# Q's zero-padded parity copies of two token groups: by GpSimd multiplies or by DMA into standing zeros

## The chip, the cores and the metric

The kernel runs on one core of one Trainium2 chip. The metric is the device time of one execution in microseconds (us), as a median of several. A profile is one further execution, recorded by the hardware profiler.

A core has engines that run side by side, each with its own queue of instructions: TensorE (PE; its weight loads stand apart as PEld), VectorE (DVE), ScalarE (ACT), GpSimd (POOL), and SyncE (SP), which here only issues DMA transfers. An engine takes its instructions strictly in order. An instruction that must wait for another engine or a transfer holds up all that stand behind it on its engine.

## What is computed

One transformer block with conditioning: a sliding-window attention branch, then a branch that mixes tokens, each behind a LayerNorm that is modulated from a vector c. There are 2048 tokens with 512 features, and the attention has 32 heads of 16 features and a window of 256.

```python
mod = (_silu(c) @ w_mod).reshape(c.shape[0], 6, 1, -1)
sa, ca, ga, sb, cb, gb = (mod[:, 0], ..., mod[:, 5])
h = _layernorm(x) * (1 + ca) + sa
# attention branch A(h)
q, k, v = (h @ wqkv) split into 32 heads of 16
scores = einsum('bhqd,bhkd->bhqk', q, k) * 16 ** -0.5
scores = where(0 <= i - j < 256, scores, -1e9)
o = einsum('bhqk,bhkd->bhqd', softmax(scores), v)
x = x + ga * (o @ wo)
h = _layernorm(x) * (1 + cb) + sb
# token-mixing branch B(h), with its own layernorm
u = gelu(einsum('bsd,sf->bdf', layernorm(h), w1) + b1)
y = einsum('bdf,fs->bds', u, w2) + b2
x = x + gb * y^T
```

## The kernel before

**Tiling.** The 2048 tokens are cut into four token groups of 512 (`tg` 0 to 3), the 32 heads into four head groups of eight (`g8` 0 to 3). A head group's Q and K are kept transposed: 128 rows (8 heads of 16 features) by 512 tokens. Attention for one token group and head group takes five units: two of kind A for the even heads, here called units 0 and 1 of the head group, one of kind C (unit 2) with the far and near corners of the window for all eight heads, and two of kind A for the odd heads. In a token group units count 5 x g8 + k, from 0 to 19.

**Why Q is there twice.** A score matmul contracts 32 rows (one of four strips of a tile, `tile_position`), and 32 rows are two heads. So that only one head counts, Q is kept in a tile `QT[tg][g8]` of 128 rows by two copies by 512 tokens: copy 0 holds the even heads with zeros in the rows of the odd ones, copy 1 the reverse. K needs no such copy. `emit_scores` (L538) reads copy 0 for the even heads, copy 1 for the odd heads, both in unit 2.

**How QT is made.** TensorE multiplies `wqkv` with `h1T` into PSUM (`dense`, L267, its matmuls bear the line L271). VectorE copies the result into a bf16 tile `qs` (L309; two buffers in turn). Then GpSimd multiplies `qs` by `mask_even` and by `mask_odd`, columns of ones and zeros by row, into the two copies (L313). The tile is allocated anew for each Q block, from a pool with two buffers for each head group. The first block of all (L511 to L523) and one half of the second are made by VectorE.

**The other pieces around it.** V goes into `VaugT` (L287), with a column of ones beside each head. The products of unit 2's probabilities read V from `Vc`, in which keys are shifted by half a block. SyncE fills it with transfers within SBUF (`copy_vc`, L631; `copies_for`, L637): two or three per head group, sent at the ends of units 0, 3, 4 and 5 of a token group. The matmuls that read it are L623. While the attention runs, SyncE also loads the first half of `w1` (`w1a`, one piece per unit from token group 1, each paced behind an exponential, L408).

**What sets the order.** The schedule is written out by hand, unit by unit (L881 to L914): the exponential of unit u (ScalarE, L598), the scores of unit u + 1, then the products of unit u - 1, and one group of dense work from `plan` (L760) whose result VectorE evacuates. Q blocks of the next token group are computed in units 13 (head group 0) and 17 (head group 1) of the group before, and those of head groups 2 and 3 in units 3 and 5 of their own. Scores are needed one unit ahead of the unit's exponential. LayerNorm steps and the like come as chains that `fill` (L723) places in VectorE's free time by a clock that the planner keeps for each engine; `evac`'s return value, 1.4 us for a Q block, tells it how long GpSimd is taken by the two multiplies (`on_pool`, L719). After the attention come the token-mixing matmuls on TensorE (L964, L1050, L1086).

Of the kernel before, what the change touches and what calls it, by code (L numbers as in the profile page):

```python
# [8 lines left out]
DT = mybir.dt  # L9
# [3 lines left out]
P = 128  # L13
# [3 lines left out]
DH = 16  # L17
# [3 lines left out]
ND = D // P  # L21
# [9 lines left out]
def kernel(  # L31
# [25 lines left out]
    dma = nc.sync  # L57
# [107 lines left out]
    build_masks()  # L165


    qpool = tc.alloc_tile_pool(name="qpool", bufs=2)
    kpool = tc.alloc_tile_pool(name="kpool", bufs=1)
    vpool = tc.alloc_tile_pool(name="vpool", bufs=1)  # L170
    qspool = tc.alloc_tile_pool(name="qspool", bufs=2)
# [7 lines left out]
    QT = [[None] * ND for _ in range(NG)]  # L179
# [13 lines left out]
    nc.gpsimd.memset(ones[:], 1.0)  # L193


    for tg in range(NG):
        VaugT[tg] = Vring[tg % 2]
        for g8 in range(ND):
            KT[tg][g8] = Kring[tg % 2][:, g8, :]

# [66 lines left out]
    def dense(out, lhsT, rhs, start, stop):  # L267

        for j in range(4):
            cols = slice(32 * j, 32 * j + 32)  # L270
            nc.tensor.matmul(  # L271
                out[cols, :], lhsT=lhsT[:, cols], rhs=rhs, start=start, stop=stop,
                tile_position=(0, 32 * j), skip_group_check=True,
            )
# [17 lines left out]
    def qk_group(tg, g8, kind, pool):  # L292
        col0 = g8 * P + (D if kind == "k" else 0)

        def mms():
            pq = pool.tile([P, 4 * P], DT.float32, name="dn")
            for dc in range(ND):
                dense(
                    pq, lhsT=wqkv[:, dc, col0 : col0 + P], rhs=h1T[tg][:, dc, :],
                    start=(dc == 0), stop=(dc == ND - 1),  # L300
                )
            return pq

        def evac(pq):
            if kind == "k":
                nc.vector.tensor_copy(out=KT[tg][g8], in_=pq[:])  # L306
                return
            qs = qspool.tile([P, 4 * P], DT.bfloat16, name="qs")
            nc.vector.tensor_copy(out=qs[:], in_=pq[:])  # L309
            QT[tg][g8] = qpool.tile([P, 2, 4 * P], DT.bfloat16, name=f"QT{g8}")  # L310
            for n, m in enumerate((mask_even, mask_odd)):
                eng = nc.vector if (tg, g8, n) == (0, 1, 0) else nc.gpsimd
                eng.tensor_scalar(  # L313
                    out=QT[tg][g8][:, n, :], in0=qs[:], scalar1=m[:], scalar2=0.0, op0=ALU.mult, op1=ALU.add,
                )
            return 0.7 if (tg, g8) == (0, 1) else 1.4
        return mms, evac, (1.05 if (tg, g8, kind) == (0, 1, "q") else 0.7)
# [70 lines left out]
    with tc.manual_schedule():  # L388
# [6 lines left out]
            out=spread[:].rearrange("p (a b) -> p a b", a=4),  # L395
            in_=identity[0:32, 0:32].unsqueeze(1).to_broadcast([32, 4, 32]),
# [52 lines left out]
        for lo, hi, in_ in (  # L449
# [3 lines left out]
                out=mask_q[:, lo:hi, :], in_=in_.to_broadcast([P, hi - lo, 64]), func=ACT.Copy,  # L453
            )
        for half in range(2):
            part64 = slice(64 - 64 * half, 128 - 64 * half)
            nc.scalar.activation(
                out=Vc[half][part64, :, 0:8, :], func=ACT.Copy,
                in_=zero[part64, 0 : 8 * 2 * DH].rearrange("p (h d) -> p h d", d=2 * DH)
# [32 lines left out]
        for dc in range(ND):  # L492
            if dc < 2:
                nc.vector.tensor_scalar(
                    out=h1T[0][:, dc, :], in0=pts[dc], scalar1=modFM[:, 4 + dc : 5 + dc],
                    scalar2=modFM[:, dc : dc + 1], op0=ALU.mult, op1=ALU.add,
                )
            else:
                nc.scalar.activation(
                    out=h1T[0][:, dc, :], in_=pts[dc], func=ACT.Identity,  # L500
# [4 lines left out]
        for dc in (0, 2, 1, 3):  # L505
            for ps, col0 in ((pq, 0), (pk, D)):
# [1 line left out]
                    ps, lhsT=wqkv[:, dc, col0 : col0 + P], rhs=h1T[0][:, dc, :],  # L508
                    start=(dc == 0), stop=(dc == ND - 1),
                )  # L510
        QT[0][0] = qpool.tile([P, 2, 4 * P], DT.bfloat16, name="QT0")  # L511

        def q_half(n, m, lo, hi):
            nc.vector.tensor_scalar(
# [545 lines left out]
    with tc.tile_pool(name="ftmp", bufs=3) as ftmp, tc.tile_pool(  # L1060
        name="ps_y0", bufs=4, space=bass.MemoryType.PSUM
# [61 lines left out]
```

## Time and profile before

| | us |
|---|---|
| median of 3 runs | 265.92 (264.77 to 267.12) |
| the profiled execution | 264.77 |
| its span in the profile | 263.0 |
| TensorE busy in it | 240.8 |
| VectorE busy | 167.2 |
| ScalarE busy | 164.3 |
| GpSimd busy | 128.6 |

Times in the profile count from the start of the span. A group line gives the source line, the engine, the operation, the tiles written and read, shapes and count, then busy time and the mean ns of one, then the idle time of the engine just before, with what ended it. The attention stage runs from about 13 to 166 us; the token-mixing matmuls follow. Busy time by stage, from the view of busy time in given windows (us):

| window | PE | DVE | ACT | POOL |
|---|---|---|---|---|
| 52 to 90 | 34.50 | 28.96 | 37.59 | 28.40 |
| 90 to 128 | 33.71 | 32.11 | 36.91 | 34.25 |
| 128 to 167 | 36.26 | 29.18 | 36.60 | 30.16 |
| 167 to 263 | 92.10 | 37.44 | 9.94 | 12.00 |

The granted clock of TensorE was 1.00 in each of them.

### The profile page before, as it was taken

The page shows a single profiled execution, that of the slowest core. Times are in us where ns is not written, and L with a number is a line of the kernel's source. Part 1 is how long each engine was busy: PE and PEld are TensorE (multiplying, and loading weights), DVE is VectorE, ACT ScalarE, POOL GpSimd, SP SyncE. Part 2 cuts the span into 40 slices and gives each one's busy share as a digit, 9 for nine tenths or more (in the row PEclk, how much of TensorE's full clock was granted, in tenths as well). Part 3 has the DMA queues.
Part 4 walks back from the last instruction along what each step waited for, and adds up shares of the span by engine and source line. Part 5 has one row for each costly group of instructions (what it writes and reads, how often), then busy time and mean ns, then how long its engine had stood idle before and what let it go on. Part 6 is the DMA issues. An engine that isn't in the chain of part 4 may idle for free.

```text
span 263.0 us, 11079 instructions
## 1 busy us (share of the span) xinstructions
PE 240.8 (92%) x4923; PEld 129.6 (49%) x4933; DVE 167.2 (64%) x353; ACT 164.3 (62%) x193; POOL 128.6 (49%) x218
## 2 busy tenths in 40 slices
PE   6988798899998879989899899999999999999994
PEld 2544455455555545555456455444444444444443
DVE  6678868875798697898786877789411001423444
ACT  6688998999999989999999999100082110000000
POOL 6104943699269998898995498954200000000000
PEclk9999979999999999999999999999999999999999
DMA  5949962134744342000122000999800000202021
GB/s 168 340 143 250 245 215 79 47 89 123 224 130 133 110 129 73 6 2 5 32 75 53 5 2 24 333 417 414 356 3 0 2 0 0 80 2 80 20 101 40
DMA packets 26084, 29.95 MB, mean 114 GB/s; under 512 B 3252, under 2 KB 23476, under 8 KB 26036
## 3 DMA queue, kind: packets, MB, share of 16 engines
q1 hardware_dynamic: 26036, 29.25, 35.4%
q8 instruction: 38, 0.62, 1.0%
q14 instruction: 10, 0.08, 0.1%
HBM read 22.55 MB, written 2.23 MB: 94 GB/s over the span
## 4 chain that ended last, share of the span: by engine, by line
PE 70%; DVE 18%; ACT 5%; issue 3%; DMA 2%; SPq 1%; ACTq 0%; DVEq 0%
PE dn L271 19%; PE py L1086 18%; PE pu L1050 8%; PE pu L964 7%; PE pss L548 5%; ACT et L598 5%; PE po L609 4%; PE po L623 3%; DVE t L655 3%; DVE qs L309 3%; DVE VaugT L287 2%; DMA wmod<-in_w_mod_dram 2%; PE pss L555 2%; DVE KT L306 2%; DVE x L370 1%
## 5 line engine op out<-in xcount | busy, mean ns | idle before, releaser
L598 ACT ACTIVATE et<-pss 128x1024 bf16<-128x1024 f32 (+1 forms) x160 | 143.8, 995 | 6.4 <-PE pss L555 5.1
L1086 PE MATMUL py<-guT,w2r 128*128 128x512 bf16 (+1 forms) x234 | 48.3, 366 | 0.2
L1065 DVE SCALAR_TENSOR_TENSOR o<-py,bFM,bc 128x512 bf16<-128x512 f32 (+1 forms) x17 | 11.7, 715 | 44.4 <-PE py L1086 44.4
L271 PE MATMUL dn<-h1T,wqkv 128*32 128x512 bf16 x496 | 33.1, 381 | 3.9 <-DVE VaugT L287 1.3
L1086 PEld LDWEIGHTS <-w2r 128*128 128x128 bf16 x238 | 23.3, 98 | 25.3
L548 PE MATMUL pss<-QT,KT 32*128 32x64 bf16 (+2 forms) x704 | 28.9, 238 | 5.8 <-ACT et L598 4.8
L655 DVE STREAM_TRANSPOSE t<-po 128x512 f32<-128x512 f32 x32 | 22.8, 711 | 11.4 <-PE po L623 11.2
L208 POOL TENSOR_TENSOR ln_rstd<-ln_ve,mhalf 128x1 f32<-128x1 f32 (+1 forms) x40 | 24.1, 602 | 5.7 <-DVE ln_ve L204 2.6
L204 POOL TENSOR_SCALAR ln_ve<-ln_mv 128x1 f32<-128x1 f32 (+1 forms) x38 | 9.1, 240 | 34.7 <-DVE ln_mv L226 17.6
L548 PEld LDWEIGHTS <-KT 32*128 32x128 bf16 x704 | 15.4, 92 | 21.3 <-issue 11.1
L609 PE MATMUL po<-et,VaugT 128*32 128x64 bf16 (+2 forms) x704 | 25.1, 241 | 0.0
L609 PEld LDWEIGHTS <-VaugT 128*32 128x32 bf16 x704 | 17.2, 96 | 11.0 <-issue 2.1
L271 PEld LDWEIGHTS <-wqkv 128*32 128x32 bf16 x512 | 13.1, 95 | 13.5 <-issue 6.0
L555 PE MATMUL pss<-mask_q,mask_k 32*128 32x256 bf16 (+1 forms) x256 | 19.2, 263 | 0.0
L667 POOL TENSOR_TENSOR merge<-t,zr 128x512 bf16<-128x512 f32 x16 | 17.0, 1060 | 3.2 <-DVE zr L666 3.2
L271 PE MATMUL dn<-wqkv,h1T 128*32 128x512 bf16 x240 | 15.7, 380 | 2.2 <-DVE VaugT L287 1.2
L975 ACT ACT_TABLE_LOAD x1 | 1.3, 1283 | 24.9 <-PE pu L964 24.9
L699 POOL TENSOR_TENSOR h<-h,bc 128x512 bf16<-128x512 bf16 x12 | 14.0, 1166 | 3.5 <-DVE h L695 3.5
L271 PE MATMUL dn<-wod,OTd 128*32 128x512 bf16 x192 | 12.6, 381 | 2.0 <-DVE KT L306 1.0
L700 POOL TENSOR_TENSOR h<-h,bc 128x512 bf16<-128x512 bf16 x12 | 13.9, 1155 | 0.9
L964 PE MATMUL pu<-hb,w1a 128*128 128x512 bf16 x58 | 13.2, 379 | 0.2 <-issue 0.2
L623 PE MATMUL po<-et,Vc 128*32 128x64 bf16 x960 | 13.0, 194 | 0.0
(113 smaller groups left out, 363.7 us busy)
## 6 DMA issues: line engine op xcount, KB each, us to landing
w2r<-in_B_w_dram SPq DMA_DIRECT2D x14, 512.0 KB, 10.1
w1a<-in_B_w_dram SPq DMA_DIRECT2D x20, 224.0 KB, 3.3
w1b<-in_B_w_dram SPq DMA_DIRECT2D x6, 448.0 KB, 7.5
Vc<-VaugT SPq DMA_DIRECT2D x32, 64.0 KB, 2.3
wmod<-in_w_mod_dram SPq DMA_DIRECT2D x8, 256.0 KB, 5.1
out_dram<-otile SPq DMA_DIRECT2D x15, 128.0 KB, 1.7
x<-in_A_x_dram SPq DMA_DIRECT2D x6, 256.0 KB, 4.2
Vc<-VaugT SPq DMA_DIRECT2D x12, 128.0 KB, 3.6
```

The source lines that it names most:

```text
L208: nc.gpsimd.tensor_tensor(out=r[:], in0=ve[:], in1=mhalf[:, 0:n], op=ALU.pow)
L271: nc.tensor.matmul(out[cols, :], lhsT=lhsT[:, cols], rhs=rhs, start=start, stop=stop, tile_position=(0, 32 * j), skip_group_check=True,)
L548: nc.tensor.matmul(pss[j // 2][:, j % 2, c0 : c0 + nq], lhsT=keys(kb, g8)[rows[j], k0 : k0 + P], rhs=QT[tg][g8][rows[j], par, q0 : q0 + nq ...
L555: nc.tensor.matmul(pss[j // 2][:, j % 2, :].rearrange("p (a r) -> p a r", a=2)[:, 0:n, :] .rearrange("p a (b q) -> p a b q", q=64)[:, :, 0 ...
L598: act = nc.scalar.activation(out=et[:, :, 0:n], in_=state.pop((u, a))[:, :, 0:n], func=ACT.Exp, scale=SCORE_SCALE,)
L609: nc.tensor.matmul(state["po"][32 * j : 32 * j + 32, q0 : q0 + nq], lhsT=VaugT[kb // 4][:, kb % 4, 8 * g8 + 2 * j + par, :], rhs=state["e" ...
L623: nc.tensor.matmul(state["po"][32 * j : 32 * j + 32, q0 : q0 + 64], lhsT=Vc[half][:, b, 8 * g8 + 2 * j + par, :], rhs=state["e", tg, g8, 2 ...
L655: nc.vector.transpose(out=state["t2"][:, par, :], in_=state["po"][:])
L667: nc.gpsimd.tensor_tensor(out=m[:].rearrange("p (b a d) -> p a b d", a=2, d=DH), in0=t2v[:, :, :, 0:DH], in1=zr[:].to_broadcast([P, 2, 16, ...
L964: nc.tensor.matmul(pu[:, i, :], lhsT=w1_of(sc, fc), rhs=hb[sc][:], start=(sc == 0), stop=(sc == NT - 1),)
L1050: nc.tensor.matmul(pu[:, i, :], lhsT=w1_of(sc, fc), rhs=hb[sc][:], start=(sc == s0), stop=(sc == NT - 1),)
L1086: nc.tensor.matmul(pys[n][:, 0 : hi - lo], lhsT=w2r[:, fc, tb * P : (tb + 1) * P], rhs=guT[fc][:, lo:hi], start=(fc == 0), stop=(fc == NF ...
```

## The change

The eight tiles QT (two rings of four head groups) are now allocated once, and token groups 0 and 2 share one ring, 1 and 3 the other. In token groups 0 and 1 the copies are made as before, so that the tiles then hold Q in the rows of one parity and zeros in the rows of the other. In token groups 2 and 3 the two multiplies are left out: SyncE sends eight transfers per Q block, one for each head (16 rows by 512 tokens, 16 KB), from `qs` into the rows and the copy where that head belongs, and the zeros of the other rows stay. `evac` returns nothing there, so the planner's clock for GpSimd does not advance. The size of the pool stays the same (eight tiles), and what is computed does too.

```diff
-    qpool = tc.alloc_tile_pool(name="qpool", bufs=2)
+    qpool = tc.alloc_tile_pool(name="qpool", bufs=1)
...
+    Qring = [[qpool.tile([P, 2, 4 * P], DT.bfloat16, name=f"QT{r}{g8}") for g8 in range(ND)] for r in range(2)]
+
     for tg in range(NG):
         VaugT[tg] = Vring[tg % 2]
+        for g8 in range(ND):
+            QT[tg][g8] = Qring[tg % 2][g8]
         for g8 in range(ND):
             KT[tg][g8] = Kring[tg % 2][:, g8, :]
...
             qs = qspool.tile([P, 4 * P], DT.bfloat16, name="qs")
             nc.vector.tensor_copy(out=qs[:], in_=pq[:])
-            QT[tg][g8] = qpool.tile([P, 2, 4 * P], DT.bfloat16, name=f"QT{g8}")
+            if tg >= 2:
+
+                for row in range(0, P, DH):
+                    head = slice(row, row + DH)
+                    dma.dma_start(out=QT[tg][g8][head, row // DH % 2, :], in_=qs[head, :])
+                return
             for n, m in enumerate((mask_even, mask_odd)):
...
-        QT[0][0] = qpool.tile([P, 2, 4 * P], DT.bfloat16, name="QT0")
```

In the changed kernel SyncE's queue has, in the places where a Q block of token groups 2 and 3 is evacuated, eight transfers more; the first of each eight waits for VectorE's copy into `qs`. Those of head group 2 stand ahead of the Vc copies of head group 1, those of head group 1, sent one token group ahead, before the Vc copies of that token group's head group 0. VectorE's later copies into `qs` wait for the transfers that read that buffer, and the score matmuls wait for the transfers where they waited for GpSimd.

## The prediction

> **What bounds the kernel now.** I read the page first, then the waits of the stretch that the change touches, then the chain of waits, then single queues. The table of instructions on the page shows what sets the pace of the attention stage: 160 exponentials on ScalarE.
>
> ```profile
> L598 ACT ACTIVATE et<-pss 128x1024 bf16<-128x1024 f32 (+1 forms) x160 | 143.8, 995 | 6.4 <-PE pss L555 5.1
> L313 POOL TENSOR_SCALAR QT<-qs,mask_odd x15: 687/692/693, 21.2 to 142.1; 128x512 bf16<-128x512 bf16 x15
> L313 POOL TENSOR_SCALAR QT<-qs,mask_even x14: 687/692/703, 24.9 to 141.4; 128x512 bf16<-128x512 bf16 x14
> ACT et L598 <- PE pss L555: 1.4, 5, 0.7
> ```
>
> The first line: 143.8 us of exponentials at 995 ns each. The next two, from the view of the tile QT (count, then minimum, median and maximum ns), are the instructions that the change removes for the last two token groups. The last, from the waits between 84 and 166 us, is the ceiling on any gain: in those 82 us ScalarE stood idle before an exponential 1.4 us in all, 0.7 of it at once. Whatever is taken off GpSimd (68.2 us busy between 84 and 165.3), the stage cannot get shorter by more than 1.4 us while 995 ns per exponential stands. After 166 us TensorE is almost alone on the chain, and nothing there is touched.
>
> The chain of waits, by its start times, gives the two ends of each distance that the change stretches:
>
> ```profile
> 96.73 0.35 PE po L623 x32
> ...
> 98.00 0.70 DVE qs L309
> ...
> 106.23 0.35 PE po L623 x32
> ...
> 134.69 0.35 PE po L623 x32
> ...
> 136.07 0.70 DVE qs L309
> ...
> 144.44 0.35 PE po L623 x32
> ```
>
> "qs L309" is VectorE's copy of a Q block, after which the zero-padded copies can be made. "po L623" are the products with Vc, which SyncE's transfers fill. At 96.73 and 134.69 they belong to head group 0, unit 2, of token groups 2 and 3; at 106.23 and 144.44 to head group 1, unit 7.
>
> The SyncE queue, from the view of the tile Vc and the timeline of SyncE:
>
> ```profile
> L633 SPq DMA_DIRECT2D Vc<-VaugT x44: 590/597/1761, 15.4 to 139.1; - x44
> DMA to landing us min/median/max: 2.0/3.3/5.6
> 1.23 1.79 SPq L116 DMA_DIRECT2D x<-in_A_x_dram  x4
> 88.31 2.87 SPq L633 DMA_DIRECT2D Vc<-VaugT  x3
> 95.00 7.03 SPq L633 DMA_DIRECT2D Vc<-VaugT  x9
> ```
>
> An issue is not free: SyncE spends 0.60 us on one Vc copy, within SBUF, and some take over a microsecond more.
>
> **What goes.** Eight Q blocks (four of token group 2, four of group 3) lose two multiplies each: 16 x 0.692 = 11.1 us of GpSimd. None of them is on the chain, and the view of the tile names nobody who waited for QT, so their removal alone is worth between 0 and the 1.4 us of ScalarE's idle time. VectorE's copy L289 (0.22 to 0.88 us for one shape) and scale L695 (0.37 to 1.20) vary when GpSimd runs beside them; the long ones at 92.36 (0.88) and 93.17 (1.20) stand just before the 0.7 us gap. The Trainium skill (SBUF — State Buffer, Who interferes with whom) has VectorE and GpSimd take turns at a shared pair of ports, held for a whole instruction; the spread of L289 agrees with it, and by that rule alone the sum would be a gain of up to 1.4 us. I take 0.3, because the merges and LayerNorm work of GpSimd stay, and because, below, the place of the large gap is held by a transfer instead.
>
> The planner, told that GpSimd is free earlier, also reorders VectorE. In the changed kernel's order one LayerNorm statistic more (0.68 + 0.18) stands before V's last copy near 94 us, and one scale more (0.37 to 1.20) near 132 us. Bounds: -0.7 (the gap goes) to +0.9 at the first, 0 to +0.4 at the second; I take 0, since at both places the next stop is a Vc copy that comes later still or leaves room.
>
> **What comes.** 64 transfers of 16 KB on SyncE, eight per Q block, waiting for qs. Issue cost of one: no row of before moves 16 partitions within SBUF. The low bound is back-to-back issues of plain rows, 1.79 / 4 = 0.45 us (L116); the high one is back-to-back Vc copies, 0.65 us (0.597 and the gap to the next). Vc costs 0.59 whether 64 or 128 KB, so size hardly matters and the kind (SBUF to SBUF) seems to; I take 0.60. Of 44 Vc copies, seven took over 1 us; eight Q issues with the three Vc copies behind them should meet one such, so 1.0 us is added per burst (0 to 2). Landing: 2.0 us, the least of the Vc row, for the smaller Q blocks and the 64 KB copies.
>
> The Trainium skill (DMA: Bandwidth & Descriptors, Rules for kernel authors) speaks against the change: it says to coalesce small transfers, since under 64 KB one pays mostly overhead. The nine Vc copies at 95.00 agree in that 64 KB cost as much issue time as 128 KB.
>
> Do the Q blocks themselves come late? Scores need the even rows of four 32-row strips, that is transfers 1, 3, 5, 7. For token group 2, head group 0, qs ends at 79.09; the seventh issue starts 6 x 0.60 + 1.0 later, 83.7, lands at 85.7; the scores began at 87.48. Head group 2: 98.70 + 4.6 + 2.0 = 105.3 against 107.38. About 2 us of cover; head groups 1 and 3 have more. Cost 0, and it would cost one for one once landing took over 4 us. The qs buffers alternate, and the block two back is about 15 us old, so VectorE's new wait for the transfers costs 0.
>
> What is queued behind the Q transfers on SyncE is what pays. Before, Vc's copies for head group 1 ran at 95.00, long before they were needed at 106.23. Now they stand behind the eight transfers of Q's head group 2, which wait for qs at 98.70. Third copy: 98.70 + 8 x 0.60 + 1.0 + 2 x 0.65 + 2.0 = 107.80, 1.57 late. Token group 3: 136.77 + 9.1 = 145.87 against 144.44, 1.43 late. For unit 2 of token group 2, Q's head group 1 is ready at 86.22 (VectorE's timeline, 85.53 + 0.69), three w1a loads (0.45 each) then precede Vc's three copies, whose own burst already had a long issue (2.87 for three): 86.22 + 4.8 + 1.0 + 1.35 + 2.3 + 2.0 = 97.67 against 96.73, 0.94 late. In token group 3 there are no loads between: 124.91 + 9.1 = 134.01 against 134.69, in time. TensorE runs about 0.4 us ahead of ScalarE (it waits 0.42 before the scores at 97.88), so each lateness loses 0.4: 1.17 + 1.03 + 0.54 = 2.74. Behind TensorE's stall stand the projections and the next scores, then the exponentials, which have no slack to win it back.
>
> Sum: +2.74 - 0.3 + 0 = +2.4. At 0.45 us per issue every place falls by 1.2, under the 0.4 of lead, and the transfers cost 0; at 0.65 three places rise by 0.4 each and the fourth stays in time, a sum of +3.6. The w1a loads (needed after 150 us) and w1b (gated by TensorE at 163) are not delayed to where they matter.
>
> The profiled execution took 264.77 (span 263.0, 1.8 around it), the fastest of three; so it becomes 267.2, and on the median, 265.92, the forecast is 268.3. What a measurement of this kernel can tell from no change is about 1%, 2.7 us.
>
> **Rivals.**
>
> *All hidden.* If one 16-partition issue costs 0.45 (plain rows, a single run each, speak for it; the constant 0.59 of every copy within SBUF against), no copy is late, and the freed GpSimd gives 0 to 1.4: 265.4. Not slower; it decides at 0.45 us per issue with one long issue per burst.
>
> *Clearly slower.* The issue costs the full 0.65, or at 0.60 each of the three bursts meets a second long one (2.74 + 3 x 1.0 - 0.3): 3.6 to 5.4 us lost at the same copies, 269.5 to 271.3. For it: the Vc row has no cheap copy within SBUF. Against: a block of 16 KB is an eighth to a quarter of Vc's.
>
> *VectorE's new order.* The moved statistic and scale delay V's last copies by 0.9 and 0.4 while the transfers hide: 267.2.
>
> *The eight transfers in series.* If each waited for the one before to land, 8 x 2.0 us (the Vc row's least) would put Q at 95.1 where 87.48 is needed, some 7.5 us late at four places: 296. Against: nine Vc copies went out in 7.03 us while each took at least 2.0 to land, so they overlap. The Trainium skill (DMA: Bandwidth & Descriptors, Anatomy of one DMA) has about 2.0 us of fixed cost in every transfer, told of GpSimd's path; the landing row agrees in size.
>
> **How the numbers follow.** Forecast 0.48; all hidden 0.28; clearly slower 0.19; VectorE's order 0.04; series 0.01. The forecast's own range, 266.9 to 269.5, straddles the 1% line at 268.6; I put 0.22 of its 0.48 above. Slower: 0.22 + 0.19 + 0.01 and 0.01 of VectorE's = 0.43. Faster by over 1% needs more than all of ScalarE's gaps: 0.03, from the spread of the runs. Same: 0.54. The range goes from the hidden case with some gain, 265.0, to the slower rival's middle, 271.0.
>
> **What would show it.** SyncE's timeline has bursts of eight Q transfers; their mean gives the issue cost (0.45, 0.60 or 0.65). The waits have "po L623" of TensorE waiting for the Vc transfer, 1 to 1.6 us at three places, and ScalarE's idle time before exponentials between 84 and 168 us grows from 1.4 to about 4. If instead the scores (L548's line) wait for a QT transfer, the landing was mis-sized; if no DMA wait shows on TensorE and the gaps stay at 1.4, all was hidden; if VectorE waits for GpSimd ahead of V's copies, it was the order.

## The result and the profile after

The changed kernel takes 273.87 us (median of 4, 272.43 to 274.69) against 265.37 (median of 4, 264.77 to 267.12) for the kernel before: a ratio of 1.0303, 95% interval 1.0232 to 1.0375. It is 8.5 us slower; the forecast had 2.4 slower and a range that ended at 271.0. Ratios, here and below, leave out single executions more than 1.5% above the fastest of their kernel; medians keep them. The profiled execution took 273.34, span 271.6 us, which is 8.6 more than the span of before.

In all profiles of the changed kernel the line numbers are shifted: the exponential is L607, the products with Vc L632, Vc's copies L642, the w1a loads L418, the new Q transfers L319, dense matmuls L276. First the page's table of instructions: the exponentials cost what they did. Then, from the waits of the attention stage's second half (84 to 178 us; columns: us in total, times, longest), where the time is.

```profile
L607 ACT ACTIVATE et<-pss 128x1024 bf16<-128x1024 f32 (+1 forms) x160 | 143.9, 997 | 13.7 <-PE pss L564 12.9
```

```profile
ACT et L607 <- PE pss L564: 9.2, 10, 4.7
PE po L632 <- DMA Vc<-VaugT: 5.4, 4, 3.2
```

ScalarE's idle time before its exponentials went from 1.4 to 9.2 us here. From the start of the first exponential to the end of the last the kernel takes 7.4 us more (151.6 before, 159.1 after), and what follows the last takes 97.7 us in both. TensorE now waits for Vc's transfers, 3.2 us at once, which it never did before, and no score matmul waits for a Q transfer. The other 1.15 us of the 8.6 stand before the first exponential (13.64 us before, 14.79 after). The change leaves the work there as it was, and the start varies from profile to profile: 13.64 and 13.87 in two of the kernel before, 13.9 to 16.5 in those of the changed kernel and its variants.

The three places are in TensorE's timeline (start, us, work, and in brackets the idle time before it with what ended it): units 2 and 7 of token group 2, unit 7 of token group 3.

```profile
100.57 0.95 PE L632 MATMUL po<-et,Vc 128*32 128x64 bf16 x32 [3.24 <-DMA Vc<-VaugT]
...
112.85 0.39 PE L632 MATMUL po<-et,Vc 128*32 128x64 bf16 x28 [0.74 <-DMA Vc<-VaugT]
...
151.95 0.21 PE L632 MATMUL po<-et,Vc 128*32 128x64 bf16 x4 [0.56 <-DMA Vc<-VaugT]
152.98 0.39 PE L632 MATMUL po<-et,Vc 128*32 128x64 bf16 x28 [0.82 <-DMA Vc<-VaugT]
```

What holds Vc back is in SyncE's timeline from 79 us on, and the price of one issue in the view of the tile QT (count, then minimum, median and maximum ns):

```profile
79.73 6.51 SPq L319 DMA_DIRECT2D QT<-qs  x8
86.35 1.96 SPq L418 DMA_DIRECT2D w1a<-in_B_w_dram  x4
88.39 5.65 SPq L319 DMA_DIRECT2D QT<-qs  x8
94.14 2.71 SPq L418 DMA_DIRECT2D w1a<-in_B_w_dram  x3
96.95 2.06 SPq L642 DMA_DIRECT2D Vc<-VaugT  x3
```

```profile
L319 SPq DMA_DIRECT2D QT<-qs x64: 507/587/1572, 79.7 to 159.4; - x64
DMA to landing us min/median/max: 1.7/2.6/4.3
```

From 79.73 to 99.0 SyncE does nothing but issue. A burst of eight takes 5.2 to 6.8 us. Four w1a loads pile up behind the first burst, so that the second one begins only at 88.39, though its `qs` was ready at 86.83. Vc's three copies come behind that. The chain of waits goes through the third of them:

```profile
97.71 0.64 SPq L642
...
98.40 2.51 DMA Vc<-VaugT
...
100.96 0.56 PE po L632 x26
101.52 1.73 PE dn L276 x15
```

The last line is a dense group that takes 1.05 us elsewhere in the stage. The view of busy time in windows (length, then busy time of PE, PEld, DVE, ACT, POOL, the granted TensorE clock, DMA share, GB/s) shows why:

```profile
100.50:101.50 1.00, 0.79 (x36) 0.62 (x40) 0.00 (x0) 0.00 (x0) 0.05 (x1) 0.50 0.89 299
101.50:102.50 1.00, 1.00 (x16) 0.32 (x8) 0.72 (x1) 0.00 (x0) 0.00 (x0) 0.50 0.40 145
102.50:103.50 1.00, 1.00 (x20) 0.29 (x16) 0.22 (x1) 0.00 (x0) 0.00 (x0) 0.50 0.02 8
103.50:104.50 1.00, 0.97 (x28) 0.44 (x22) 1.00 (x2) 0.42 (x1) 0.00 (x0) 0.80 0.00 0
```

After the stall TensorE has work but half its clock, for about 3.4 us. The 3.24 us of TensorE become a gap of 4.72 on ScalarE.

### The profile page after: what moved, and what is told of

It is laid out like the page before. It is cut to its first block, busy times and chain, and to the rows that moved or that the text cites. A ratio compares the mean times of both kernels' runs of the same rounds, so it can differ in the third digit from the quotient of the medians.

```text
span 271.6 us, 11180 instructions
## 1 busy us (share of the span) xinstructions
PE 243.5 (90%) x4933; PEld 129.4 (48%) x4933; DVE 167.0 (61%) x353; ACT 164.4 (61%) x193; POOL 117.8 (43%) x202
## 4 chain that ended last, share of the span: by engine, by line
PE 63%; DVE 16%; DMA 7%; ACT 4%; issue 3%; SPq 3%; POOL 2%; ACTq 0%; DVEq 0%
PE py L1095 18%; PE dn L276 16%; PE pu L1059 8%; PE pu L973 7%; PE pss L557 4%; ACT et L607 4%; DMA Vc<-VaugT 3%; PE po L618 3%; PE po L632 3%; DVE t L664 2%; DMA wmod<-in_w_mod_dram 2%; DVE qs L314 2%; DVE VaugT L292 2%; DMA QT<-qs 2%; DVE ln_stats L692 2%
## 5 line engine op out<-in xcount | busy, mean ns | idle before, releaser
L607 ACT ACTIVATE et<-pss 128x1024 bf16<-128x1024 f32 (+1 forms) x160 | 143.9, 997 | 13.7 <-PE pss L564 12.9
L276 PE MATMUL dn<-h1T,wqkv 128*32 128x512 bf16 x496 | 33.9, 388 | 4.0 <-DVE VaugT L292 1.7
L557 PE MATMUL pss<-QT,KT 32*128 32x64 bf16 (+2 forms) x704 | 29.5, 239 | 5.7 <-ACT et L607 4.8
L276 PEld LDWEIGHTS <-wqkv 128*32 128x32 bf16 x512 | 13.1, 97 | 13.9 <-issue 6.6
L632 PE MATMUL po<-et,Vc 128*32 128x64 bf16 x960 | 13.7, 196 | 5.5 <-DMA Vc<-VaugT 5.4
L276 PE MATMUL dn<-wqkv,h1T 128*32 128x512 bf16 x240 | 15.7, 381 | 1.8 <-DVE VaugT L292 0.9
L708 POOL TENSOR_TENSOR h<-h,bc 128x512 bf16<-128x512 bf16 x12 | 13.9, 1154 | 6.1 <-DVE h L704 6.1
L276 PE MATMUL dn<-wod,OTd 128*32 128x512 bf16 x192 | 12.6, 381 | 2.6 <-DVE qs L314 1.1
L632 PEld LDWEIGHTS <-Vc 128*32 128x32 bf16 x960 | 10.0, 98 | 8.2 <-DMA Vc<-VaugT 6.5
```

Of the source, the lines that this page charges most:

```text
L276: nc.tensor.matmul(out[cols, :], lhsT=lhsT[:, cols], rhs=rhs, start=start, stop=stop, tile_position=(0, 32 * j), skip_group_check=True,)
L557: nc.tensor.matmul(pss[j // 2][:, j % 2, c0 : c0 + nq], lhsT=keys(kb, g8)[rows[j], k0 : k0 + P], rhs=QT[tg][g8][rows[j], par, q0 : q0 + nq ...
L607: act = nc.scalar.activation(out=et[:, :, 0:n], in_=state.pop((u, a))[:, :, 0:n], func=ACT.Exp, scale=SCORE_SCALE,)
L632: nc.tensor.matmul(state["po"][32 * j : 32 * j + 32, q0 : q0 + 64], lhsT=Vc[half][:, b, 8 * g8 + 2 * j + par, :], rhs=state["e", tg, g8, 2 ...
```

## The experiments

Theory 1 is that the loss is SyncE's issue time: Vc's copies (and loads) queue up behind the bursts of Q transfers. Theory 2 has Q itself late. Theory 3 has the planner's new order of VectorE and GpSimd at fault. A fourth would be that the transfers cost something wherever they stand in the queue. Ratios are against runs of the kernel before on the same chip, with 95% intervals.

| kernel | transfers, per burst | us | ratio |
|---|---|---|---|
| multiplies removed, nothing in their place | 0 | 265.85 | 1.0011 (0.9984 to 1.0039) |
| half by transfer | 32, 4 | 265.49 | 1.0012 (0.9990 to 1.0034) |
| token group 3 only | 32, 8 | 267.55 | 1.0074 (1.0037 to 1.0112) |
| six of eight by transfer | 48, 6 | 268.20 | 1.0101 (1.0066 to 1.0137) |
| changed kernel, repeated | 64, 8 | 273.41 | 1.0281 (1.0205 to 1.0357) |
| changed, planner told 1.4 us | 64, 8 | 274.94 | 1.0361 (1.0270 to 1.0451) |
| changed, w1a loaded early | 64, 8 | 274.74 | 1.0342 (1.0295 to 1.0390) |
| the same, repeated | 64, 8 | 273.49 | 1.0311 (1.0229 to 1.0393) |
| changed, bursts behind Vc | 64, 8 | 269.06 | 1.0123 (1.0062 to 1.0185) |
| bursts behind Vc, w1a early | 64, 8 | 267.25 | 1.0057 (1.0027 to 1.0086) |
| transfers cut in two | 128, 16 | 310.64 | 1.1703 (1.1663 to 1.1743) |

**The removal alone.**

```diff
             if tg >= 2:
-                for row in range(0, P, DH):
-                    head = slice(row, row + DH)
-                    dma.dma_start(out=QT[tg][g8][head, row // DH % 2, :], in_=qs[head, :])
                 return
```

> Leaves out, for token groups 2 and 3, both the zero-padded copies of Q and their transfers (scores are computed from the Q of two groups earlier). So it shows the removal by itself. Theory 1 (the loss comes from Vc's copies queued behind the Q transfers on SyncE): 264.0 to 265.4 us, TensorE waits for no Vc transfer, ScalarE idle before the exponentials at most 1.4 us. Theory 2 (Q itself comes late): the same. Theory 3 (the planner's new order of VectorE and GpSimd costs the time; the order here is that of the changed kernel): 270 to 274 us, and the gaps stay.

Measured 265.85 us, ratio 1.0011; Theory 1 had given 265.4 at most. Taking 11.1 us of multiplies off GpSimd is worth nothing that can be measured, and costs nothing. The planner's order is that of the changed kernel here, so the order isn't what costs 8 us.

**The planner told the old figure.**

```diff
-                return
+                return 1.4
```

> The transfers stay; the planner is told the old 1.4 us of GpSimd per Q block, so that it orders VectorE and GpSimd as before the change. Theory 1: no gain, 272 to 275 us, with the products with Vc waiting for their transfers at units 2 and 7 as in the changed kernel. Theory 3: back to 266 to 269 us.

Measured 274.94 us: no gain, so Theory 3 falls a second time. The waits between 84 and 178 us are those of the changed kernel:

```profile
ACT et L607 <- PE pss L564: 9.1, 9, 3.0
PE po L632 <- DMA Vc<-VaugT: 6.6, 7, 2.0
```

**The same transfers, later in the queue.** `evac` only notes the block. The transfers are issued at the end of the unit, behind that unit's Vc copies, even heads first; those noted in unit 17 wait for the end of the next token group's unit 0, behind its Vc copies.

```diff
-                for row in range(0, P, DH): ...
+                late.append((tg, g8, qs))
...
                 copies_for(tg, max(ul - 2, 0))
+            if ul not in (17, 18, 19):
+                while late:
+                    t_, g_, q_ = late.pop(0)
+                    for row in list(range(0, P, 2 * DH)) + list(range(DH, P, 2 * DH)):
+                        head = slice(row, row + DH)
+                        dma.dma_start(out=QT[t_][g_][head, row // DH % 2, :], in_=q_[head, :])
```

> All 64 transfers stay, 8 per Q block and as long; each burst is only put into SyncE's queue behind the Vc copies that are needed first, instead of ahead of them, and the strips that the scores need first go first. Theory 1: 264.5 to 266.5 us, no wait of TensorE for a Vc transfer over 0.5 us. Theory 2 (Q late): 273 us or more, since Q is now later. Theory 3 (order on VectorE and GpSimd): 273 us. A theory by which the transfers themselves disturb others (memory traffic, SyncE's time): 270 or more.

Measured 269.06 us: of the 8.5, 4.8 are gone with the order alone. TensorE waits for no Vc transfer any more, which only Theory 1 expected. But it isn't the 264.5 to 266.5 that Theory 1 gave. SyncE's timeline, here with Vc at L640 and Q at L848:

```profile
91.27 2.76 SPq L640 DMA_DIRECT2D Vc<-VaugT  x3
94.08 6.47 SPq L848 DMA_DIRECT2D QT<-qs  x8
100.65 1.44 SPq L416 DMA_DIRECT2D w1a<-in_B_w_dram  x2
102.19 2.04 SPq L640 DMA_DIRECT2D Vc<-VaugT  x3
104.33 6.86 SPq L848 DMA_DIRECT2D QT<-qs  x8
111.29 4.89 SPq L640 DMA_DIRECT2D Vc<-VaugT  x6
116.28 11.65 SPq L848 DMA_DIRECT2D QT<-qs  x16
```

Between 91.27 and 127.9 SyncE issues almost without a pause, so whatever comes last is late. Now it is Q, by little, as the waits between 84 and 178 us say:

```profile
ACT et L605 <- PE pss L562: 3.1, 8, 0.7
...
PEld L555 <- DMA QT<-qs: 1.1, 2, 0.7
```

ScalarE's gaps are 3.1 us, 1.7 over those of before. This profile's span, 267.0, is 4.0 above that of before. Beside these gaps, it has its first exponential late, at 16.47 us instead of 13.64: the granted clock was 0.5 from 10.83 to 14.24 us. One profile can't tell how much of the median's 3.6 us lies there.

**w1a's loads early.** The piled-up loads at 86.35 and 94.14 suggested them as the cause of the largest stall.

```diff
-            for sc, n in [x for x in [next(w1box.get("sc", iter(())), None)] if x]:
+            for sc, n in [x for x in [next(w1box.get("sc", iter(())), None) for _ in range(2)] if x]:
```

> The loads of w1a go out two per unit and so are done before the first Q burst; nothing else changes. Theory 1: the 4.7 us gap at unit 2 of token group 2 goes (the w1a loads held up by the first burst were what pushed the second one, and Vc behind it, back), TensorE's half-clock spell there with it, and the time falls to about 269.3 (268.5 to 270.3); the waits at units 7 stay. If the w1a loads played no part there: 273.

Measured 274.74 us: a miss. The stall at unit 2 did go, but unit 7 of token group 2 grew from 0.74 to 2.83 us (TensorE's timeline):

```profile
110.86 0.21 PE L632 MATMUL po<-et,Vc 128*32 128x64 bf16 x4 [0.94 <-DMA Vc<-VaugT]
112.95 0.39 PE L632 MATMUL po<-et,Vc 128*32 128x64 bf16 x28 [1.89 <-DMA Vc<-VaugT]
```

ScalarE's gap at unit 7 of token group 3 went from 1.34 to 2.10, and around a half-clock spell near 78 us stand 2.2 us of new gaps. So each of the two kernels was profiled again, to see how much of this changes from one execution to the next.

> The changed kernel once more, for a second profile of the same code. If the 4.7 us at unit 2 of token group 2 and the 0.75 and 1.34 us at the two units 7 belong to the order of the queue alone, they come back within 0.5 us each. If each place's loss is partly a draw (whether an issue that takes over a microsecond, or a straggling piece of a landing, falls into it), the sum of ScalarE's gaps after 84 us stays near 9 us while its parts move by 1 to 2 us: unit 2 between 2.5 and 4.7, units 7 between 0.7 and 2.9. Time 272 to 276 us in both cases.

> The kernel with w1a's loads two per unit once more, for a second profile. Its first took the wait at unit 2 away and yet 274.7 us, with 2.2 us of gaps at 77 to 82 us (a half-clock spell lay there) and 2.80 and 2.10 us at the units 7. If the gaps at 77 us were the spell's, they are under 1 us here unless a spell falls there again, and the fastest runs come near 271; if early loads cost time there by themselves, they come back. If a saved wait at unit 2 is always paid again at unit 7, the units 7 together are 4 to 5 us here again and in the repeated changed kernel under 3.

273.41 and 273.49 us. In the repeated changed kernel ScalarE's gaps after 84 us are 7.7 in all: 2.77 and 0.91 at unit 2, 0.26 and 1.38 at the units 7, so unit 2's loss, 1.0 us smaller, and that of token group 3's unit 7 come back and the third is smaller. With early w1a they are 6.7: none for Vc at unit 2, but 2.60 and 1.69 at the units 7, and no spell at 78 us. Of about 3.7 us saved at unit 2, 2.65 are paid at the units 7, and four runs of each, spread over 5 to 6 us, show no difference in time. Why is argued, not shown: a stall at unit 2 also puts off everything that comes later, ScalarE and so the next need of Vc, while SyncE works on. In three profiles without early w1a the gap at token group 2's unit 7 was 0.3, 0.8 and 2.2 us, in two with it 2.6 and 2.8. How much of that comes from where long issues (below) happen to fall stays open.

**The kernel before, a second profile.** Its text asks whether the half-clock spell is the stall's.

> The kernel before once more, for a second profile. If the half-clock spell of TensorE (3.4 us; at 34 us in the profile of before, at 102 in that of the changed kernel) is a thing of its own that falls anywhere, it stands at another place here, and the first exponential begins between 13.6 and 16.5 us; if the stall at unit 2 of the changed kernel called it up, it stands at about 34 us again and the first exponential at 13.6. Either way the time is 264.5 to 267.2 us, and the stretch from the first exponential's start to the last one's end about 151.6 us (159.1 in the changed kernel).

264.70 us. No spell at all this time; first exponential at 13.87; from its start to the end of the last 151.3 us (159.1 in the changed kernel). So a spell also comes without the change and then costs little. The section on the hardware returns to it.

**Half, and six of eight.** The odd strips go by transfer, the even ones by one multiply of GpSimd; then six strips by transfer and one multiply on 64 partitions.

```diff
-                for row in range(0, P, DH):
+                for row in range(DH, P, 2 * DH):
                     head = slice(row, row + DH)
...
+                nc.gpsimd.tensor_scalar(
+                    out=QT[tg][g8][:, 0, :], in0=qs[:], scalar1=mask_even[:], scalar2=0.0, op0=ALU.mult, op1=ALU.add,
+                )
-                return
+                return 0.7
```

> Only the four odd strips of each Q block go by transfer, the even ones by GpSimd's multiply as before: half the issues on SyncE, half of the time taken off GpSimd. Theory 1 (issues queued ahead of Vc): each burst is 2.6 us shorter, so the third Vc copy at unit 7 lands 1 to 2.6 us earlier than its need and the waits go: 265.0 to 267.5 us. If every transfer, and not the queue, costs a fixed share of the loss: half of 8.5 us, about 269.7.

> Six of eight strips by transfer, the other two by one multiply of GpSimd on 64 partitions: a burst of 3.8 us of plain issues. The prediction put the point at which no copy is late at eight issues of 0.45 (3.6 us) with a long one of 1.0 on top; if that working holds with the measured 0.64, six issues are just at the edge: 265.3 to 267.0 us, with ScalarE's gaps after 84 us at 1.1 to 2.5. If the loss were in proportion to the transfers: 271.8; if it grew evenly from four to eight: 269.7.

265.49 and 268.20 us. With four transfers per burst nothing is lost. SyncE's timeline has bursts of 2.4 to 3.1 us here. Vc's copies for unit 2 (L645) start 3.6 us earlier than in the changed kernel, though this profile's first exponential is 1.6 us later. ScalarE's gaps between 84 and 178 us are below those of before:

```profile
81.56 3.11 SPq L319 DMA_DIRECT2D QT<-qs  x4
84.77 3.39 SPq L421 DMA_DIRECT2D w1a<-in_B_w_dram  x4
88.72 2.42 SPq L319 DMA_DIRECT2D QT<-qs  x4
91.25 2.06 SPq L421 DMA_DIRECT2D w1a<-in_B_w_dram  x3
93.39 2.05 SPq L645 DMA_DIRECT2D Vc<-VaugT  x3
```

```profile
ACT et L610 <- PE pss L567: 1.1, 6, 0.2
```

With six, both waits of token group 2 are back (TensorE's timeline, products with Vc at L636); 268.20 is above the range expected:

```profile
98.72 0.21 PE L636 MATMUL po<-et,Vc 128*32 128x64 bf16 x4 [1.30 <-DMA Vc<-VaugT]
99.12 0.39 PE L636 MATMUL po<-et,Vc 128*32 128x64 bf16 x28 [0.19 <-DMA Vc<-VaugT]
...
109.85 0.39 PE L636 MATMUL po<-et,Vc 128*32 128x64 bf16 x28 [0.82 <-DMA Vc<-VaugT]
```

**Bursts of eight in token group 3 alone** (`if tg >= 3:`).

> Transfers in bursts of eight for token group 3 only: 32 transfers, as many as in the half experiment, but each burst as long as in the changed kernel. Theory 1 (length of the burst ahead of Vc decides): the wait at unit 7 of token group 3 comes back (0.5 to 2 us), perhaps one at unit 2 (the bursts of head groups 0 and 1 stand back to back), so 266.3 to 268.5 us, against 265.5 with bursts of four in both groups. If the number of transfers decides: 265.5.

267.55 us: as many transfers as in the half experiment, but 2 us more. Number alone doesn't decide, length does. The wait at unit 7 of token group 3 is back, in the changed kernel's size; unit 2 has one of 0.53 us:

```profile
146.49 0.21 PE L632 MATMUL po<-et,Vc 128*32 128x64 bf16 x4 [0.56 <-DMA Vc<-VaugT]
147.53 0.39 PE L632 MATMUL po<-et,Vc 128*32 128x64 bf16 x28 [0.82 <-DMA Vc<-VaugT]
```

**Twice the transfers, the same bytes.**

```diff
-                    dma.dma_start(out=QT[tg][g8][head, row // DH % 2, :], in_=qs[head, :])
+                    for half in (slice(0, 2 * P), slice(2 * P, 4 * P)):
+                        dma.dma_start(out=QT[tg][g8][head, row // DH % 2, half], in_=qs[head, half])
```

> Each transfer cut in two by columns: 128 issues of 8 KB, the same bytes. Theory 1: if an issue costs 0.64 us at 8 KB too, a burst takes 10 to 12 us, and SyncE, with its 12 Vc copies of 0.68, has some 50 us to issue in a token group of 38.5: it becomes the bound, 285 to 300 us. If the bytes or the landing make the loss, not the number of issues: 273 to 275 us.

310.64 us, beyond even what Theory 1 expected. The view of the tile QT, and the waits between 84 and 215 us:

```profile
L320 SPq DMA_DIRECT2D QT<-qs x128: 513/587/1701, 79.6 to 199.6; - x128
DMA to landing us min/median/max: 1.7/1.8/3.5
```

```profile
ACT et L608 <- PE pss L565: 42.2, 15, 10.7
...
PE po L633 <- DMA Vc<-VaugT: 25.7, 8, 9.2
...
PE pss L558 <- DMA QT<-qs: 7.5, 5, 2.2
```

An issue of 8 KB costs the same 587 ns as one of 16 KB. Landing is no slower, so it is neither bytes nor landing that hold the kernel up, but the number of issues. Against the changed kernel the 64 issues more cost 36.8 us, 0.57 each, nearly an issue's own time. Now scores wait for Q transfers too, 7.5 us. The expectation took SyncE's issue time alone. What made the time longer still isn't separated: SyncE stood still for 3.8 and 4.6 us (ahead of 113.17 and 173.03), and TensorE's mean granted clock was 0.928.

**Both remedies together**, the bursts behind Vc and w1a early:

> All 64 transfers, put into the queue behind the Vc copies that are needed first (as in the order experiment), and w1a's loads two per unit, so that they are done before the first burst. In the order experiment SyncE issued without a pause from 91 to 128 us and Q's last block of token group 2 came 0.7 us late; without w1a in between, Theory 1 expects no wait of TensorE for a transfer in the attention stage, ScalarE's gaps after 84 us at 1.4 to 2.5 us and 265.0 to 267.5 us. If the transfers cost something beside the queue's order (memory traffic on the cores' buffers, GpSimd's and VectorE's new order): 268.5 or more, as in the order experiment.

267.25 us, within the time expected, and still 0.57% above before (0.27 to 0.86). But one wait for a Q transfer of 0.8 us is left after 84 us where none was expected, and ScalarE's gaps there are 3.0, above the 1.4 to 2.5 given. So the order of the queue, w1a's loads included, accounts for most of the loss, and a small cost of the transfers themselves is not excluded. Sending them from another engine's queue, which would leave SyncE's as it was, was not tried. No version tried beats the kernel before: the half version equals it, and with the removal alone worth nothing there is little to win.

## Why the prediction was off

**Right.** ScalarE's 1.4 us as a ceiling of any gain: the removal alone gave none (0.3 had been taken). Zero for the planner's order. Zero for Q's own lateness: no score waited. The three places where Vc comes late and the fourth in time: TensorE waits for Vc at those three and nowhere else. The loss at unit 7 of token group 3, forecast 1.03, came as 1.34 and 1.38 in two profiles. That the eight transfers overlap: eight go out in 5.2 to 6.8 us while each takes 1.7 us or more to land.

**The issue cost** was taken at 0.60 and is the high bound: 0.587 and the gap to the next, 0.64. With the one long issue counted per burst this hardly matters: eight bursts measured 48.1 us in SyncE's timeline (a pause of 0.3 is in it), 6.0 each, against 5.8 forecast.

**The step that failed is the sum for unit 2 of token group 2**, "86.22 + 4.8 + 1.0 + 1.35 + 2.3 + 2.0 = 97.67 against 96.73, 0.94 late", which lost 0.54. It lets the burst begin when its `qs` is ready. It leaves out that the burst of head group 0, a head group earlier, holds SyncE's queue too, and that the w1a loads it holds up go out in one piece ahead of the next burst. Counted from its `qs`, the third copy was to land 11.45 us later and landed 14.08 later (86.83 to 100.91). Of these 2.63, 1.56 are the burst's late start (88.39), 1.46 the three loads (2.81 with the gap instead of 1.35), and -0.34 the copies themselves. The burst itself is 0.05 shorter than forecast. So 0.94 late became a stall of 3.24.

**The price of a stall** was its length less TensorE's lead. The granted clock fell to half after this one, so the next dense group took 1.91 us instead of 1.05 and the Vc products 0.95 instead of 0.42: 1.4 us more, which no term had. The prediction gave the place 0.54 and ScalarE's gap there is 4.72.

**Places were added as if independent.** Unit 7 of token group 2 was to lose 1.17; the three profiles have 0.3 to 2.2, and 2.6 to 2.8 when unit 2 doesn't stall. The reading, argued and not shown, is that a queue which is behind passes its lateness on, so that its cost is set by the whole stretch. By that the rival "clearly slower", 269.5 to 271.3, had the right mechanism too, with the wrong lever: its range came from 0.65 an issue and more long ones, not from the backlog.

**Two small gaps had no term**: 0.38 and 0.35 us of ScalarE at 110.11 and 149.65 us. Ahead of them a dense group of TensorE waits 0.46 and 0.43 us for VectorE's copy of head group 3's Q. Their cause isn't separated; the profile of the half version has no gap over 0.23 us after 84 us. The gain of 0.3 taken for the removal didn't come.

## What to carry to other kernels

Before moving work to a DMA queue, add up that queue's issue time over the whole stretch, with everything that already stands in it. Here 0.64 us an issue, and a long one now and then, made 5.2 to 6.8 us per Q block on a queue that held copies with a due time. Four issues per block cost nothing, six 1%, eight 3%, sixteen 17%. As long as what stands behind still lands before it is due, the queue is free; from eight to sixteen nearly every added issue was paid in full. Order the queue by due time, and prefer few large transfers to many small ones, since an issue cost the same from 8 to 128 KB here.

## What the runs showed of the hardware

**Small transfers within SBUF cost their issue, not their bytes**: 587 ns in the median for 8 KB and for 16 KB, about 0.6 for Vc's 64 and 128 KB. The Trainium skill (DMA: Bandwidth & Descriptors, Issuing engines are not separate DMA queues) calls the time to initiate a DMA usually small relative to the DMA itself. These rows differ for a burst: one issue is 0.59 us against a landing of 1.8 us (8 KB) or 2.6 us (16 KB) in the median, so a quarter or a third of it, and the landings overlap while the issues don't. Eight issues take 5.1 us, longer than one landing.

**Long issues meet instruction fetches.** Between 79 and 163 us of the changed kernel's profile 14 issues of SyncE took over 0.98 us, and each overlaps in time with a 16 KB transfer on the instruction queue, of which there were 18. An example, a w1a load at 94.14 that took 1.76 us, from the view of DMA traffic between 94 and 96 us:

```profile
q8 instruction: 1, 0.02, 4.3%
```

Single pieces of a landing can be late too: in the kernel with early w1a a Vc copy issued at 109.45 had 15 of 16 pieces by 2.0 us and the last at 3.46, TensorE waited for it, and an instruction transfer ran in that stretch as well. This may be why single places differ by 1 to 2 us between profiles of one kernel. That the instruction transfer causes the long issue or the late piece is read from the coincidence alone; no run shows it.

**A half clock after a stall.** In all three profiles of the changed kernel and its twin with the old planner figure, the granted clock was 0.5 for about 3.4 us after unit 2's stall of 2.4 to 3.2 us. The Trainium skill (TensorE: Matmul & The Clock Gate, What's actually happening) has the clock throttled after an idle window of about 3.4 us, by a window that runs freely. The length agrees, and within each profile the times between the clock's changes are multiples of 3.41 us (92.16, 3.41 and 167.25 in the changed kernel's). But the stalls were shorter than that, and with early w1a stalls of 2.6 and 2.8 us at unit 7 brought no spell. Cut by these multiples, the 3.41 us just before the three spells had TensorE busy for 0.25, 1.28 and 1.48 us, and the stretches with the other two stalls for at least 1.57 us. So where a stall falls seems to count. It isn't the whole rule, since 1.64 us came before the spell at 77.7 us, and which stall pays is not settled here. Spells also come in the prologue, without such a stall: the two latest first exponentials, at 16.41 and 16.47 us, go with one. Two profiles should not be compared to a microsecond before that is looked at.
